# A small exp, its norm and its transpose taken one pass earlier in a fused attention and gated-MLP kernel

## Chip, cores, metric

The kernel runs on one core of one Trainium2 chip. The time is device time in microseconds (us) of that core; runs of each kernel are compared. The runs were made on several chips, so times are compared only within the same rounds, by their ratio. A span in a profile is about 1.8 us shorter than the time of the same run. Where a landing time of a DMA is given to 0.01 us, it is read from the records of the trace; the views round the time from issue to landing to 0.1 us.

The five engines are TensorE (PE, with weight loads as PEld), VectorE (DVE), ScalarE (ACT), GpSimd (POOL) and SyncE (SP), which here only issues DMAs. All DMAs of the part studied are issued by SP on one queue, which feeds 16 DMA engines.

## The reference

Attention without a softmax over scores: q is normalised over its 64 columns, k over the sequence, then two small products. The result, with the heads side by side, goes through a two-layer MLP with a scaled Silu.

```
q_s = softmax(q, axis=-1)                  # q, k, v: batch 8, heads 8, sequence 576, 64 columns
k_s = softmax(k, axis=sequence)
kv  = einsum('bhsd,bhse->bhde', k_s, v)
x   = einsum('bhsd,bhde->bhse', q_s, kv)   # turned into 4608 tokens x 512
h   = x @ w_in                             # 512 x 2048
out = (h * sigmoid(beta * h)) @ w_out      # 2048 x 512
```

## The kernel before

The 4608 tokens are worked off in nine slabs of 512. Slabs 0 to 7 are the first 512 rows of each batch. The 64 rows that remain of each batch (the "remaining queries", QRF when loaded, EQR after exp, QTR once transposed) are handled two batches at a time and gathered for slab 8. A slab has a first pass (`x @ w_in`, Silu on ScalarE, 64 matmuls) and a second pass (`@ w_out`, 64 matmuls). The attention of the next batch is slipped between these matmuls at fixed places: `spread(steps, a, b)` puts steps between the matmuls of positions a to b.

ScalarE needs one function table for Exp and one for Silu. So the exps of coming batches are bundled at the end of a first pass. The parts that the change touches:

```python
def load_qrem(b):                       # remaining queries of batches b and b+1
    i = b // 2 % 2
    for h in range(2):
        a = bass.AP(qt_h, (b + h)*H*S*D + SM*D, [[D, SR], [S*D, H], [1, D]])   # 256 B pieces
        add(SP, lambda e, h=h, a=a: e.dma_start(QRF[i][64*h:64*h+64, :, :], a), ...)

def load(b):
    load_main("qf", qt_h, QF, b); load_k(b); load_v(b)    # 1.05 + 1.18 + 1.18 MB
    if b % 2:
        load_qrem(b - 1)                                  # 0.26 MB

def exp_qr(pi):   ...   # ScalarE: EQR = exp(QRF)
def norm_rem(pi): ...   # VectorE: reduce, reciprocal, multiply
def tr_dma(pi):   ...   # SP: dma_start_transpose(QTR, EQR)

# slab 0, between the passes
load(2)
load_qrem(0)
...
# slab 0, end; slab 1's first matmuls are already mixed in
o2_evac(0, 2, 5, ACTE)
<Silu table load>
at(0, 0, 3); out_now(1, 2, 7, DVE); ...; out_now(1, 3, 7, DVE); at(2); at(3)
o2_evac(0, 3, 6, DVE)
store(0)
load(3)
# ... rest of slab 1's first pass: Silu on ScalarE ...
# slab 1, before the second pass
exp_qr(0)               # loads the Exp table
norm_rem(0)
tr_dma(0)
for b in (2, 3): exp_q(b); exp_k(b); ...
# slab 1, second pass: the remaining queries of batches 0 and 1 are used here
todo = spread(outr_steps(1), 101.5, 103) + attn_late(2)
```

`outr_steps(1)` are eight short matmuls that read QTR. They stand in TensorE's order, so TensorE waits there if QTR has not come.

The softmax here doesn't subtract the row's maximum and nothing guards it: scores larger than these inputs give would overflow.

## Time and profile before

| | before |
|---|---|
| median, first three runs | 285.29 us (284.43 to 285.29) |
| span of the profile | 283.1 us |
| TensorE busy | 275.2 us, 97% |
| TensorE's wait for QTR | one, near 68 us |

From the profile's page of the kernel before: the first part (busy us, share of the span, instructions) and the first line of the part on the chain of work that ended last.

```profile
PE 275.2 (97%) x1559; PEld 136.0 (48%) x1589; DVE 117.3 (41%) x218; ACT 178.6 (63%) x243; POOL 38.6 (14%) x57
...
PE 90%; ACT 4%; DMA 3%; issue 1%; DVE 1%; SPq 0%; ACTq 0%
```

TensorE is the limit almost everywhere. What can be won is only what TensorE loses in stalls. The chain of waits of the kernel before, from 55 to 71 us, shows the largest one left (columns: start in us, length in us, what).

```profile
55.05 4.28 PE PS L366 x19
...
60.05 1.28 ACT L322
...
61.35 0.64 ACT EQR L322
...
62.01 0.70 DVE QRS L340
...
62.97 0.69 DVE EQR L343
...
63.69 4.35 DMA QTR<-EQR
...
68.08 2.58 PE PS L366 x42
```

The chain leaves TensorE at 59 us, goes through the Exp table load, exp, norm and transpose, and returns to TensorE at 68.08. TensorE's timeline of the kernel before around that point (start, length, engine, line, operation, shapes, count, and the idle time before it):

```profile
64.76 2.75 PE L366 MATMUL PS<-WOUT,GT 128*128 128x512 bf16 x11
68.08 0.26 PE L366 MATMUL PS<-QTR,KVD 128*128 128x64 bf16 x3 [0.57 <-DMA QTR<-EQR]
```

The bracket counts idle time after the modelled end of the last matmul. Counted from start to start, where a matmul of 512 columns takes 0.216 us, the stall is 0.73 us. In what follows "stall" means this count. The SP queue and ScalarE of the kernel before, from their timelines:

```profile
33.42 0.43 SPq L249 DMA_DIRECT2D QF<-in_q_dram  x1
...
41.74 4.48 SPq L266 DMA_DIRECT2D QRF<-in_q_dram  x2
48.89 0.37 SPq L716 DMA_DIRECT2D out_dram<-O2S  x1
...
54.13 5.35 SPq L266 DMA_DIRECT2D QRF<-in_q_dram  x2
63.69 1.29 SPq L456 DMA_TRANSPOSE QTR<-EQR  x1
```

```profile
46.19 1.28 ACT L825 ACT_TABLE_LOAD   x1
...
48.87 3.58 ACT L642 ACTIVATE GT<-PS,BETA 128x512 bf16<-128x512 f32 x6 [1.18 <-PE PS L366]
```

ScalarE has 1.18 us to spare in front of slab 1's first Silu. On SP, the QRF load at 54.13 is the tail of load(3), and the transpose is next behind it. Load(3) landed at 67.47, the transpose at 68.03. Of the last piece of load(3), the QRF load issued at 57.20, the view of the QRF tile from 57.18 to 58 us says:

```profile
DMA to landing us min/median/max: 10.3/10.3/10.3
```

### The profile page before, as it was taken

Reading aid. Unit: us, or ns where it says so; the run is one execution under the profiler, and the core shown is the slowest. Engines: PE = TensorE matmul, PEld = TensorE weight load, DVE = VectorE, ACT = ScalarE, POOL = GpSimd, SP = SyncE. Lnnn points to the kernel's source line nnn. Section 1 sums busy time; section 2 is a strip of 40 time slices with the busy share of each in tenths; the row PEclk is TensorE's granted clock in tenths of the full one; section 3 lists DMA queues with packets and bytes.
Section 4 is the critical chain, followed back from the end, with each engine's and each line's share of the span. In section 5 each row is a group of like instructions: output and inputs, shape, how many; then the busy total and the mean of one; then the engine's idle time right before and its main releaser. Section 6 shows DMA issues by size and latency. Waiting matters only on the chain.

```text
span 283.1 us, 3884 instructions
## 1 busy us (share of the span) xinstructions
PE 275.2 (97%) x1559; PEld 136.0 (48%) x1589; DVE 117.3 (41%) x218; ACT 178.6 (63%) x243; POOL 38.6 (14%) x57
## 2 busy tenths in 40 slices
PE   7899999999999999999999999999999999999995
PEld 3545454444455445544554445444544444444443
DVE  4864886029781348124841473055705300110012
ACT  5968687999968926795579636892660076017500
POOL 6522041308021032100130000000000000000000
PEclk9999999999999999999999999999999999999999
DMA  7999999998998998217980033002500030012022
GB/s 243 375 391 400 389 387 378 347 382 138 336 322 251 362 365 285 39 35 252 375 102 1 0 150 74 2 1 100 141 2 0 9 141 0 0 54 96 0 74 74
DMA packets 41466, 50.07 MB, mean 177 GB/s; under 512 B 20324, under 2 KB 28772, under 8 KB 40296
## 3 DMA queue, kind: packets, MB, share of 16 engines
q1 hardware_dynamic: 40496, 48.77, 53.7%
q10 hardware_dynamic: 952, 1.06, 1.1%
q8 instruction: 12, 0.20, 0.3%
q14 instruction: 6, 0.05, 0.0%
HBM read 36.71 MB, written 9.44 MB: 163 GB/s over the span
## 4 chain that ended last, share of the span: by engine, by line
PE 90%; ACT 4%; DMA 3%; issue 1%; DVE 1%; SPq 0%; ACTq 0%
PE PS L366 89%; ACT EK L317 2%; DMA KF<-in_k_dram 2%; DMA QTR<-EQR 2%; ACT L322 0%; SPq L249 0%; PE PS L364 0%; ACT GT L642 0%; DVE QRS L340 0%; DVE EQR L343 0%; ACT VB L351 0%; ACT EQR L322 0%; ACT XT L530 0%; ACT O2S L710 0%; DVE O2S L731 0%
## 5 line engine op out<-in xcount | busy, mean ns | idle before, releaser
L642 ACT ACTIVATE GT<-PS,BETA 128x512 bf16<-128x512 f32 x144 | 96.6, 689 | 79.0 <-PE PS L366 79.0
L366 PE MATMUL PS<-WOUT,GT 128*128 128x512 bf16 (+2 forms) x579 | 131.4, 373 | 0.7 <-issue 0.2
L366 PE MATMUL PS<-XT,WIN 128*128 128x512 bf16 x561 | 131.2, 379 | 0.5
L366 PEld LDWEIGHTS PS<-XT,WIN 128*128 128x128 bf16 x576 | 60.1, 106 | 59.3 <-POOL WIN L566 0.5
L366 PEld LDWEIGHTS PS<-WOUT,GT 128*128 128x128 bf16 x592 | 55.3, 98 | 62.0 <-DVE O2S L710 0.2
L710 DVE COPY O2S<-PS 128x512 f32<-128x512 f32 x33 | 22.7, 687 | 107.7 <-PE PS L366 107.7
L366 PE MATMUL PS<-VB,EK 128*128 128x65 bf16 (+2 forms) x306 | 35.8, 191 | 1.2 <-ACT VB L351 0.7
L351 POOL CAST VB<-VF 128x576 bf16<-128x576 f32 x30 | 22.7, 757 | 76.5 <-DMA VF<-in_v_dram 47.1
L307 ACT ACTIVATE EK<-KF 64x1152 bf16<-64x1152 f32 x24 | 27.8, 1157 | 0.4
L366 PEld LDWEIGHTS PS<-VB,EK 128*128 128x128 bf16 x306 | 22.0, 98 | 8.1 <-ACT VB L351 0.8
L332 DVE TENSOR_REDUCE QS<-EQ 128x8 f32<-128x512 bf16 (+1 forms) x22 | 20.1, 913 | 3.1 <-ACT EQ L295 2.9
L441 DVE CAST XT<-PS 128x512 bf16<-128x512 f32 x24 | 16.4, 690 | 10.9 <-PE PS L366 10.9
L295 ACT ACTIVATE EQ<-QF 128x512 bf16<-128x512 f32 x32 | 17.9, 619 | 3.0 <-DMA QF<-in_q_dram 2.8
L334 DVE TENSOR_TENSOR EQ<-EQ,QI 128x1024 bf16<-128x1024 bf16 (+1 forms) x15 | 16.9, 1128 | 0.5
L366 PE MATMUL PS<-QT,KVD 128*128 128x512 bf16 x30 | 11.4, 379 | 0.0
L317 ACT ACTIVATE EK<-KF 64x576 bf16<-64x576 f32 (+1 forms) x12 | 9.9, 839 | 1.8 <-DMA KF<-in_k_dram 1.7
L334 POOL TENSOR_TENSOR EQ<-EQ,QI 128x512 bf16<-128x512 bf16 x7 | 7.3, 1042 | 18.5 <-DVE QI L333 18.2
L403 DVE TENSOR_TENSOR KVD<-PS,RC 64x64 bf16<-64x64 f32 (+2 forms) x28 | 8.6, 308 | 1.3 <-PE PS L364 0.5
L340 DVE TENSOR_REDUCE QRS<-EQR 128x8 f32<-128x512 bf16 x4 | 2.7, 678 | 13.2 <-ACT EQR L322 13.2
L366 PE MATMUL PS<-XT 128*128 128x512 f32 x10 | 6.7, 801 | 1.5 <-DVE XT L219 1.5
L642 ACT ACT_TABLE_LOAD x5 | 6.4, 1283 | 0.1
L295 ACT ACT_TABLE_LOAD x5 | 6.4, 1283 | 0.1
(52 smaller groups left out, 77.5 us busy)
## 6 DMA issues: line engine op xcount, KB each, us to landing
out_dram<-O2S SPq DMA_DIRECT2D x8, 1024.0 KB, 4.6
KF<-in_k_dram SPq DMA_DIRECT2D x6, 1152.0 KB, 8.2
VF<-in_v_dram SPq DMA_DIRECT2D x6, 1152.0 KB, 11.4
QF<-in_q_dram SPq DMA_DIRECT2D x6, 1024.0 KB, 6.8
KF<-in_k_dram SPq DMA_DIRECT2D x8, 288.0 KB, 8.1
VF<-in_v_dram SPq DMA_DIRECT2D x8, 288.0 KB, 8.7
WST<-in_moe_w_in_dram SPq DMA_DIRECT2D x8, 256.0 KB, 7.8
O2S<-in_moe_w_in_dram SPq DMA_DIRECT2D x4, 512.0 KB, 11.9
```

Of the source, the lines that this page charges most:

```text
L295: add(ACTE, lambda e, o=o, a=a: e.activation(o, a, ACT.Exp), r=[("qf", i, hp)], w=[("eq", i, hp)])
L307: add(ACTE, lambda e, o=o, a=a: e.activation(o, a, ACT.Exp), r=[("kf", i, h) for h in hps], w=[("ek", i, h, e_) for h in hps])
L317: add(ACTE, lambda e: e.activation(o, a, ACT.Exp), r=[("kf", i, h) for h in hps], w=[("ek", i, h, e_) for h in hps])
L332: add(DVE, lambda e: e.tensor_reduce(s_, a, AX.X, ALU.add), r=ks, w=[("qs", i, hp0)])
L334: add(eng, lambda e: e.tensor_tensor(a, a, vb, ALU.mult), r=ks + [("qi", i, hp0)], w=ks)
L340: add(DVE, lambda e: e.tensor_reduce(QRS[:, :], EQR[i][:, :, :], AX.X, ALU.add), r=[("eqr", i)], w=["qrs"])
L351: add(eng, lambda e: (e.copy if eng == ACTE else e.tensor_copy)(o, a), r=[("vf", i, hp), ("vone", i)], w=[("vb", i, hp, h) for h in ((0, 1 ...
L366: add(PE, lambda e: e.matmul(o, l, r_, start=start, stop=stop), r=r, w=w, bank=[bk])
L403: add(DVE, lambda e, o=o, a=a, s_=s_: e.tensor_tensor(o, a, s_, ALU.mult), r=[("ps", bk)] + [("rc", i, h) for h in hps], w=[("kvd", i, h, ...
L441: add(eng, lambda e: (e.copy if eng == ACTE else e.tensor_copy)(XT[i][:, hp, :], PS[bk][:, :]), r=[("ps", bk)], w=[("xt", i, hp)], bank=[bk])
L642: add(ACTE, lambda e: e.activation(GT[:, f, :], PS[bk][:, :], ACT.Silu, scale=BETA[:, f:f + 1]), r=[("ps", bk), "beta"], w=[("gt", f)], ba ...
L710: add(eng, lambda e: (e.copy if eng == ACTE else e.tensor_copy)(O2S[t % 2][:, u, :], PS[bk][:, :]), r=[("ps", bk)], w=[("o2", t % 2, u)], ...
```

## The change

The intent: the exp of the remaining queries of batches 0 and 1 no longer stands in front of the transpose in slab 1's second pass. It is taken earlier, while ScalarE still has the Exp table, so that norm and transpose can be done during slab 1's first pass. For that, the remaining queries must arrive earlier, so their load goes ahead of load(2).

```diff
             if t == 0:
+                load_qrem(0)
                 load(2)
-                load_qrem(0)
 ...
                 o2_evac(0, 2, 5, ACTE)
+                exp_qr(0)
                 <Silu table load>
 ...
                 o2_evac(0, 3, 6, DVE)
+                norm_rem(0)
                 store(0)
                 load(3)
+                tr_dma(0)
                 continue
 ...
             if t == 1:
                 nb = [2, 3]
-                exp_qr(0)
-                norm_rem(0)
-                tr_dma(0)
```

No instruction is added or dropped. On ScalarE the exp moves, on SP the two loads move; the order on TensorE, VectorE and GpSimd is the same.

## The prediction

> **What bounds the kernel now.** TensorE. The page has PE busy 275.2 us of a 283.1 us span (97%); the chain that ended last is 90% PE. From 20 us on, the starts of consecutive matmuls follow each other at their own pace (0.216 us for 512 columns; steps of double length are missing records). The stalls left are 0.1 us at 39.8, 0.1 at 53.08 (a PSUM bank waiting for Silu) and 0.73 us at 68.08, where the first QTR matmul waits for the transposed remaining queries.
>
> **What the change aims at.** That stall. In the chain of waits its path is: Exp table load at 60.05 (1.28 us), exp of EQR 61.35 (0.64), norm on VectorE 62.01 to 63.66, DMA transpose issued 63.69, landed 68.03 (4.35 us). The change takes exp, norm and issue out of this path. It can save at most 0.73 us, 0.26%.
>
> **Costs, from the trace.** No instruction is added: the orders show two moves, the 0.61 us exp on ScalarE and two QRF loads on the SP queue; both table loads (1.28 us) stay.
> - exp_qr(0) in front of the Silu table: ScalarE gets there at 46.19 and the first Silu waits until 48.87 for PE, with 1.18 us idle. The 0.61 us fits, with about 0.55 us to spare, if QRF has landed by about 46.7. QRF is now issued at 33.4; the transfer ahead of it landed at 43.92, and 1024 packets of 256 B add about 1 to 2 us (estimate from packets of 18 to 36 ns, 64 to an engine): about 45.3. No stall expected; beyond 46.7 PE pays in full: the bank wait at 53.08 has no slack.
> - norm_rem (1.65 us) falls into 13.2 us of VectorE idleness (48.9 to 62.0): free.
> - ScalarE's exps in slab 1's second pass start 0.6 us earlier, VectorE's norms about 1.7 us earlier, both transposes of batch 2 and load(4) likewise. No matmul waits for them now.
>
> **Why I expect little of the 0.73 us.** The transpose is still behind load(3) on the one SP queue. The Trainium skill (DMA: Bandwidth & Descriptors, section "Queues, rings and completion order") says each DMA engine consumes descriptors in ring order. The trace agrees: load(3)'s last piece (QRF of batch 2, issued 57.20) landed at 67.47 and the transpose 0.56 us later, though issued 3.8 us before that; packet records show the early engines' transpose packets held from 65.7 to 67.32, for the slowest engine. The fastest of these four transposes landed in 2.4 us, which would be 66.1. So the loads bound it, not its issue. After the change it is issued at about 59.5, when load(3) is issued, at the same place in the queue; the bytes ahead are the same, so it lands at about 67.5 to 68.1 again.
>
> **Predicted:** 284.9 us, 8 in 10 between 284.2 and 285.8 (before: runs 284.43 to 285.29). Faster by over 2%: 0.005; within 2%: 0.985; slower: 0.01.
>
> **What would show it.** QRF landing near 45 us and no ScalarE wait longer than before at 46 to 49; QRS right after O2S at 49 us; transpose issued near 59.5 with 8 us or more to landing; the QTR matmul still stalling 0.4 to 0.8 us near 68; batch 2's transposes issued 1.5 us earlier.
>
> **What would make it wrong.** The transpose passing the loads or the slowest DMA engine lagging less (up to 0.7 us gained); QRF landing after 46.7 us (loss); a transpose waiting early in the rings disturbing load(3).

## The result and the profile after

| | before | after |
|---|---|---|
| median of 6 runs | 285.24 us (284.43 to 285.64) | 285.50 us (284.94 to 286.02) |
| ratio after / before, 95% interval | | 1.0014 (0.9995 to 1.0034) |

A ratio is the mean time of one kernel's runs over that of the other's of the same rounds, so it is not quite the ratio of the medians. A second set (five rounds, `a_again` below) gave 1.0003 (0.9989 to 1.0018). The change brings nothing that can be told from zero.

The page of the kernel after, first and fourth part:

```profile
PE 276.1 (97%) x1559; PEld 136.3 (48%) x1589; DVE 117.2 (41%) x218; ACT 178.9 (63%) x243; POOL 38.5 (14%) x57
...
PE 94%; DMA 3%; issue 1%; ACT 0%; DVE 0%
```

The chain of waits after, 55 to 71 us:

```profile
59.73 0.69 ACT GT L642
...
60.48 8.45 DMA QTR<-EQR
...
68.98 2.08 PE PS L366 x32
```

Table load, exp and norm are gone from the chain. The stall is not: the one DMA now fills the whole stretch, 8.45 us from issue to landing where it was 4.35. The piece in front of it in the chain is only what SP happened to follow. TensorE's timeline after:

```profile
64.71 3.19 PE L366 MATMUL PS<-WOUT,GT 128*128 128x512 bf16 x13
68.98 0.20 PE L366 MATMUL PS<-QTR,KVD 128*128 128x64 bf16 x1 [1.09 <-DMA QTR<-EQR]
```

The stall, start to start, is 1.25 us. The SP queue, ScalarE and VectorE after:

```profile
33.84 4.24 SPq L266 DMA_DIRECT2D QRF<-in_q_dram  x2
38.12 2.69 SPq L249 DMA_DIRECT2D QF<-in_q_dram  x1
...
49.27 0.36 SPq L716 DMA_DIRECT2D out_dram<-O2S  x1
...
53.58 6.86 SPq L266 DMA_DIRECT2D QRF<-in_q_dram  x2
60.48 3.98 SPq L456 DMA_TRANSPOSE QTR<-EQR  x1
```

```profile
45.65 1.04 ACT L710 COPY O2S<-PS 128x512 f32<-128x512 f32 x2
46.77 0.63 ACT L322 ACTIVATE EQR<-QRF 128x512 bf16<-128x512 f32 x1
47.42 1.28 ACT L826 ACT_TABLE_LOAD   x1
...
49.25 3.00 ACT L642 ACTIVATE GT<-PS,BETA 128x512 bf16<-128x512 f32 x5 [0.33 <-PE PS L366]
```

```profile
49.27 0.69 DVE L340 TENSOR_REDUCE QRS<-EQR 128x8 f32<-128x512 bf16 x1
...
50.23 0.69 DVE L343 TENSOR_TENSOR EQR<-EQR,QRI 128x512 bf16<-128x512 bf16 x1
```

Everything moved as meant. The exp fits in front of the Silu table and the first Silu still waits for TensorE. The norm is done at 50.92 us. But SP comes to the transpose only after it has issued load(3), at 60.48, and the transpose then lands 0.57 us behind load(3)'s last piece (68.37). Before, it landed 0.56 us behind it. Of this last piece, issued at 58.11, the view of the QRF tile from 58.08 to 59 us says:

```profile
DMA to landing us min/median/max: 10.3/10.3/10.3
```

To compare profiles whose starts differ by some tenths of a microsecond, the table below counts from a fixed matmul, the last output product of batch 1 in slab 0 (47.15 us before, 47.53 us after). Where QTR is there in time, its first matmul starts 20.2 us after that point (20.20 and 20.21 us in four runs below without a wait).

| profile | order of the first QRF loads | load(2) and QRF ended | load(3) ended | QTR landed | stall, us |
|---|---|---|---|---|---|
| before | behind load(2) | 7.22 | 20.32 | 20.89 | 0.73 |
| b_again | behind | 6.90 | 19.62 | 20.21 | under 0.1 |
| after | ahead of load(2) | 7.82 | 20.84 | 21.41 | 1.25 |
| a_again | ahead | 7.54 | 20.48 | 21.02 | 0.86 |
| b_qrem_first | ahead | 7.60 | 20.67 | 21.27 | 1.11 |

From the fixed matmul to the end of the span, less this stall, the five profiles took 235.25 to 235.33 us. So behind this point the stall accounts for the difference between them to within 0.1 us. The part ahead of it varies by itself by 0.4 us (47.14 to 47.55), which also moves the times.

### The profile page after: what moved, and what is told of

Same layout as the page of the kernel before. It is cut to its first block, busy times and chain, and to the rows that moved or that the text cites. A ratio compares the mean times of both kernels' runs of the same rounds, so it can differ in the third digit from the quotient of the medians.

```text
span 284.0 us, 3884 instructions
## 1 busy us (share of the span) xinstructions
PE 276.1 (97%) x1559; PEld 136.3 (48%) x1589; DVE 117.2 (41%) x218; ACT 178.9 (63%) x243; POOL 38.5 (14%) x57
## 4 chain that ended last, share of the span: by engine, by line
PE 94%; DMA 3%; issue 1%; ACT 0%; DVE 0%
PE PS L366 93%; DMA QTR<-EQR 3%; PE PS L364 1%; ACT GT L642 0%; DVE XT L219 0%; DVE O2S L731 0%; DVE KVD L403 0%; ACT L295 0%
## 5 line engine op out<-in xcount | busy, mean ns | idle before, releaser
L351 POOL CAST VB<-VF 128x576 bf16<-128x576 f32 x30 | 22.7, 756 | 79.5 <-PE PS L366 49.9
L366 PE MATMUL PS<-XT 128*128 128x512 f32 x10 | 7.7, 908 | 1.5 <-DVE XT L219 1.5
L295 ACT ACT_TABLE_LOAD x6 | 7.7, 1283 | 0.1
L642 ACT ACT_TABLE_LOAD x5 | 6.4, 1283 | 0.1
L366 PE MATMUL PS<-QTR,KVD 128*128 128x64 bf16 x32 | 5.2, 193 | 1.1 <-DMA QTR<-EQR 1.1
```

Source lines behind the costliest of these rows:

```text
L295: add(ACTE, lambda e, o=o, a=a: e.activation(o, a, ACT.Exp), r=[("qf", i, hp)], w=[("eq", i, hp)])
L351: add(eng, lambda e: (e.copy if eng == ACTE else e.tensor_copy)(o, a), r=[("vf", i, hp), ("vone", i)], w=[("vb", i, hp, h) for h in ((0, 1 ...
L366: add(PE, lambda e: e.matmul(o, l, r_, start=start, stop=stop), r=r, w=w, bank=[bk])
L642: add(ACTE, lambda e: e.activation(GT[:, f, :], PS[bk][:, :], ACT.Silu, scale=BETA[:, f:f + 1]), r=[("ps", bk), "beta"], w=[("gt", f)], ba ...
```

## Experiments

Three explanations were on the table. *Queue order*: the transpose is held by the bytes queued ahead of it. *Issue*: its landing follows the moment it is issued. *Traffic*: a transpose must wait until load traffic on the DMA engines has ended, wherever it stands in the queue. Names beginning with a_ are edits of the changed kernel, those with b_ of the kernel before. One slip in the expectations: where they speak of batch 1's third output product as the fixed point, it is the fourth and last one; the numbers are those of the table above.

### The transpose ahead of load(3)

```diff
                 norm_rem(0)
+                tr_dma(0)
                 store(0)
                 load(3)
-                tr_dma(0)
```

> The changed kernel with one edit: the transpose of the remaining queries is put on the SP queue ahead of the store of slab 0 and of load(3), instead of behind them. Queue-order theory (the transpose is held by the bytes queued ahead of it): it is issued near 51 us, lands at 55 to 57.5 us behind load(2) alone, the QTR stall near 68 us (0.73 us before, 1.25 us after in the profiles) is below 0.1 us, and the time is 0.5 to 1.2 us under the changed kernel, about 284.5 us. Batch 2's own transposes, still behind load(3), become the next to wait for, but need not come before 71 us. Rival (a transpose has to wait until the load traffic on the DMA engines has ended, wherever it stands in the queue): it lands no earlier than about 67 us and the stall stays at 0.5 us or more. Second rival (a transpose among loads holds up the loads that follow): load(3) lands over 1 us later than 68.4 us.

Measured: 284.53 us (284.11 to 284.85), ratio to before 0.9979 (0.9962 to 0.9996), and 0.64 us under the changed kernel of the same rounds (285.17). The SP timeline of this kernel:

```profile
50.95 1.29 SPq L456 DMA_TRANSPOSE QTR<-EQR  x1
52.29 0.57 SPq L716 DMA_DIRECT2D out_dram<-O2S  x1
...
56.20 4.86 SPq L266 DMA_DIRECT2D QRF<-in_q_dram  x2
65.66 4.53 SPq L451 DMA_TRANSPOSE QT<-EQ  x2
```

The transpose landed at 55.66 us, 4.7 us after its issue, amid full load traffic and 0.38 us behind load(2)'s last piece (55.28), and the stall is gone: TensorE's waits no longer name QTR. So traffic alone does not hold a transpose until 68 us. The second rival came true as well: load(3) ended at 69.77 us, 1.4 us later than in the first profile after. No matmul waited for it. How much of that is the transpose and how much the store and loads issued 3 us later is not separated here. The same edit is not possible in the kernel before, whose exp comes too late for it.

### The changed kernel and the kernel before once more

> The changed kernel once more, unedited, for a second profile and timing beside the others. Queue-order theory: the transpose lands 0.4 to 0.7 us behind the last load(3) piece, wherever that falls; the stall follows the slowest DMA engine and lies between 0.4 and 1.5 us. Time 285.0 to 285.9 us, 0 to 0.3% over the kernel before. If the change itself had slowed something, the stall or another wait would again be larger than the 0.73 us of before.

Measured: 285.17 us (284.95 to 285.37), ratio 1.0003. Stall 0.86 us, the transpose 0.54 us behind load(3).

> The kernel before, unedited, for a second profile. Queue-order theory: the transpose lands 0.4 to 0.7 us behind the last piece of load(3) again; the stall differs from 0.73 us by no more than the landing of load(3) does. It shows how much of the difference between stalls of 0.73 and 1.25 us is chance.

Measured in one look: the transpose landed at 67.77 us, 0.59 us behind load(3) (67.18), and TensorE hardly waited (under 0.1 us). So the stall of the kernel before is itself a matter of some tenths: 0.73 us in one profile, nearly none in another. The landing behind load(3) is the fixed part: 0.49 to 0.60 us in the seven profiles that keep the whole of load(3) right ahead of the transpose.

### The QTR matmuls later in TensorE's order

```diff
-                todo = spread(outr_steps(1), 101.5, 103) + attn_late(2)
+                late = attn_late(2)
+                kv01, rest = late[:18], late[18:]
+                todo = spread([s for _, s in kv01[:17]], 101.5, 104) + \
+                    spread(outr_steps(1), 104.1, 105.4) + [(105.45, kv01[17][1])] + rest
```

They cannot go further down, because the 18th step is followed by writes to the KVD tile that they read.

> The kernel before with the QTR matmuls moved by about 1.1 us down TensorE's order (behind 17 of the 18 steps of batch 2's first two key-value products), nothing on other engines moved. If the stall near 68 us is nothing but a wait for the transpose's landing, TensorE gets to these matmuls at 68.2 us or later, the stall shrinks to below 0.3 us and the time falls by 0.4 to 0.7 us against the kernel before, to about 284.6 us. Rival (the wait only moves on: exps or transposes of batch 2 then come too late): a new stall of 0.4 us or more at the key-value or output products of batch 2 between 68 and 74 us, and no gain.

Measured: 284.34 us (284.24 to 284.48), ratio 0.9974 (0.9960 to 0.9989). TensorE's timeline of this kernel:

```profile
68.37 0.38 PE L366 MATMUL PS<-WOUT,GT 128*128 128x512 bf16 x1
68.58 0.34 PE L366 MATMUL PS<-QTR,KVD 128*128 128x64 bf16 x6
68.76 0.38 PE L366 MATMUL PS<-WOUT,GT 128*128 128x512 bf16 x1
```

The transpose landed at 67.50; TensorE came to it at 68.58 and did not wait. No new stall appeared. Of all kernels run here this one has the lowest ratio to the kernel before, without moving anything on another engine.

### Only the new order of loads

```diff
             if t == 0:
+                load_qrem(0)
                 load(2)
-                load_qrem(0)
```

> The kernel before with only the changed order of loads: the two loads of the remaining queries ahead of load(2); exp, norm and transpose stay where they were. In four profiles so far load(2) with these two loads ended 6.9 to 7.2 us after a fixed matmul (batch 1's third output product) where they came last, and 7.5 to 7.8 us where they came first, and load(3) ended 19.6 to 20.3 against 20.5 to 20.8 us after it. If the new order itself costs this load time (the many 256-byte packets slow the engine that lags), load(2) ends at 7.4 to 7.9 and load(3) at 20.3 to 20.9 us here too, and the stall is as after, 0.6 to 1.3 us, with a time of 0.0 to 0.2% over the kernel before. Rival (chance, or the earlier issue of the transpose behind load(3)): load ends as in the kernel before, stall 0 to 0.75 us.

Measured: 285.62 us (284.62 to 286.01), ratio 1.0025 (1.0006 to 1.0044). Load(2) with QRF ended at 7.60, load(3) at 20.67, stall 1.11 us. The time is a little more than the expected 0.0 to 0.2%. So the reordering of loads makes load(2) and load(3) end later by itself, with exp, norm and transpose left where they were. All twelve profiles agree: load(2) with QRF ended 6.90 to 7.37 us after the fixed matmul in the six of the old order, 7.44 to 7.82 in the six of the new one. For load(3), where the whole of it stood right ahead of the transpose on the one queue, it is 19.62 to 20.34 in four profiles of the old order and 20.48 to 20.84 in three of the new one, a gap of only 0.14 us. In the total time the cost is at the edge of the noise: the changed kernel, with the same order, gave 1.0014 and 1.0003. The stretches view (columns: stretch, its length, busy time of each engine with instruction counts, TensorE clock, DMA share, GB/s moved) of the kernel before, and of this one, over the same two stretches:

```profile
41.50:46.50 5.00, 4.95 (x39) 2.50 (x39) 3.35 (x10) 4.71 (x9) 1.33 (x2) 1.00 1.07 365
50.00:54.50 4.50, 4.50 (x22) 2.11 (x21) 0.00 (x0) 4.50 (x9) 0.66 (x1) 1.00 1.14 328
```

```profile
41.50:46.50 5.00, 4.95 (x39) 2.49 (x39) 3.35 (x10) 4.57 (x8) 1.33 (x2) 1.00 1.15 270
50.00:54.50 4.50, 4.50 (x22) 2.10 (x21) 0.00 (x0) 4.50 (x9) 0.00 (x0) 1.00 1.06 414
```

Wherever the QRF pieces of 256 bytes run, the last column falls: 365 to 270 GB/s when they come early, and in the second stretch 414 to 328 when they come late. The sums do not quite cancel: 3.30 MB moved before (365 x 5.0 + 328 x 4.5) and 3.21 MB here. The packet records of this run show other packets slowed beside them: from 42.0 to 44.5 us, in means of half a microsecond, those of 2304 bytes took 0.15 to 0.18 us in place of 0.10, and those of 1024 bytes 0.07 to 0.10 in place of 0.05. The last packets of 2304 bytes of load(2), with no 256-byte pieces beside them, took 0.09 (53.0 to 54.5 us). Why the loss is larger with QRF ahead than behind is not settled.

### The new exp without the new order of loads

```diff
             if t == 0:
-                load_qrem(0)
                 load(2)
+                load_qrem(0)
```

> The changed kernel without the reordering of loads: the remaining queries of batches 0 and 1 come behind load(2) again, while their exp stays in front of the Silu table. They land near 54 us, 7 us after the third output product of batch 1, so ScalarE waits from 46.2 to about 54 us in front of slab 1's first Silu, which starts near 56.5 us in place of 48.9. TensorE, whose PSUM banks have no slack here (0.1 us stall at 53.1 us already), loses 6.5 to 8 us: time 291 to 293.5 us, 2.2 to 2.9% slower. It shows what the reordering buys. If TensorE had slack in its eight banks, the loss would be under 5 us. The QTR stall is gone, as TensorE comes later.

Measured: 294.10 us (293.75 to 294.50), ratio 1.0325 (1.0309 to 1.0341), more than expected. ScalarE's timeline, TensorE's waits (us in total, times, longest) and three stretches of this kernel:

```profile
54.69 0.63 ACT L322 ACTIVATE EQR<-QRF 128x512 bf16<-128x512 f32 x1 [8.42 <-DMA QRF<-in_q_dram]
```

```profile
PE PS L366 <- ACT GT L642: 6.7, 2, 5.1
```

```profile
20.00:52.00 32.00, 31.61 (x187) 15.73 (x189) 19.63 (x46) 20.00 (x29) 6.38 (x7) 1.00 1.07 383
57.40:64.80 7.40, 5.54 (x13) 1.82 (x15) 0.00 (x0) 5.55 (x11) 0.00 (x0) 0.50 1.10 358
70.00:100.00 30.00, 29.78 (x205) 15.36 (x208) 19.35 (x36) 26.55 (x34) 9.53 (x11) 1.00 0.78 233
```

ScalarE waits 8.42 us for QRF, and TensorE, out of free PSUM banks, waits 6.7 us for Silu. The rest is the clock: when TensorE went on after 5.1 idle us, its granted clock was 0.50 for 7.4 us more, and matmuls started 0.43 us apart in place of 0.216. The 13 recorded ones cost about 2.7 us more (13 x 0.21, an estimate, as records can be missing). 6.7 and 2.7 give 9.4 us; the medians differ by 9.3. (The QTR stall, which is gone here, is not taken off, so the sum is good to some tenths only.) The Trainium skill (TensorE: Matmul & The Clock Gate, section "Part 1: The HAM clock gate (the "warmup" mystery)") says that an idle window of about 3.4 us halves the clock until TensorE has been busy for about as long. In this trace the clock record falls to 0.50 at 54.63 us, 2.3 us after the last matmul ended (52.37), which is sooner than that, though no matmul ran then to confirm it. It returns to 1.00 at 64.87, 3.9 us after matmuls went on at 60.93 behind a second idle piece of 1.6 us, which agrees. The early loads are thus a necessary part of the change.

### Fewer bytes ahead of the transpose

Both kernels were run without the load of V of batch 3, 1.18 MB ahead of the transpose (the expectations write 1.15). The result is wrong (batch 3 uses batch 1's V).

```diff
-            load_v(b)
+            if b != 3:
+                load_v(b)
```

> The changed kernel without the load of V of batch 3, 1.15 MB ahead of the transpose in the queue (a wrong result on purpose: batch 3 uses batch 1's V). Queue-order theory: everything behind it comes forward by the 2.8 to 3.2 us that these bytes take, so the transpose, issued near 60 us, lands at 65 to 66.2 us in place of 68.2 to 68.9, and the stall is gone. Rival (it lands when some other thing near 68 us frees it, not the bytes): it still lands after 67 us.

> The kernel before without the load of V of batch 3 (a wrong result on purpose, as above). Here the queue has emptied, or nearly, when the transpose is issued at 63.7 us, so now its issue decides: it lands 2.4 to 3 us after that, at 66.0 to 66.7 us, up to 1 us later than in the changed kernel without V. So the change does bring the landing forward where no backlog holds it. Rival (bytes do not matter): 67.5 us or later.

The SP lines of the view of the QTR tile between 45 and 75 us, with the time to landing, for the changed kernel and for the kernel before, each without V:

```profile
L457 SPq DMA_TRANSPOSE QTR<-EQR x1: 3477/3477/3477, 57.2 to 57.2; - x1
...
DMA to landing us min/median/max: 7.6/7.6/7.6
```

```profile
L457 SPq DMA_TRANSPOSE QTR<-EQR x1: 1291/1291/1291, 63.7 to 63.7; - x1
...
DMA to landing us min/median/max: 2.5/2.5/2.5
```

In the changed kernel the transpose landed at 64.85 us, 0.57 us behind load(3), which ended at 64.28. It was issued early and still waited for what was ahead. In the kernel before the queue had emptied at 64.27, and the transpose landed at 66.19, 2.5 us after its issue. Here the issue decides, and by itself the change does bring the landing forward, by 1.2 us counted from the fixed matmul (17.79 against 19.02). Both stalls are gone, and both landings are those of the queue-order theory to within 0.2 us of the stated ranges. This is the case that the change was made for; with V loaded it does not arise.

### The transpose on ScalarE's queue

```diff
-        def tr_dma(pi):
+        def tr_dma(pi, eng=SP):
 ...
                 load(3)
-                tr_dma(0)
 ...
                 nb = [2, 3]
+                tr_dma(0, ACTE)
```

Batch 2's first transpose also waits for QTR here, so that no two transposes from different queues are under way at once.

> The changed kernel with the transpose of the remaining queries issued by ScalarE on its own queue, at the end of slab 1's first pass (about 60.2 us, as late as in the changed kernel), instead of behind load(3) on the SP queue; batch 2's first transpose waits for it, so that no two are under way at once. Queue-order theory (its place in the SP queue holds it, not the traffic as such): it passes what is left of load(3), lands at 63 to 66 us, and the QTR stall near 68 us is gone; time 0.3 to 1.2 us under the changed kernel, less up to 1 us if the issue holds up ScalarE's exps of batch 2. Rival (a transpose needs all 16 DMA engines to have finished the loads under way, from whichever queue): it lands no earlier than 67 us and the stall stays at 0.4 us or more.

Measured: 284.95 us (284.77 to 285.12), ratio to before 1.0010 (0.9995 to 1.0025). From the view of the QTR tile of this kernel:

```profile
L457 ACTq DMA_TRANSPOSE QTR<-EQR x1: 1485/1485/1485, 59.5 to 59.5; - x1
...
DMA to landing us min/median/max: 8.2/8.2/8.2
```

Neither expectation was met in full. The landing came as late as the rival had it (67.70 us), but it was ahead of load(3)'s end (68.49), so the transpose did pass the tail of the SP queue. It needed 8.2 us for that, and the stall shrank to 0.23 us, between the two expectations. No gain in time is to be seen: the ratio is no better than the changed kernel's 1.0014 and 1.0003 of other rounds. The packet records show where the 8.2 us went. The transpose's first packet ran at 63.77 us, 4.2 us after its issue (1.3 us in the kernel before without V, where the queue was empty); what held it until then is open. Then several of its packets were held at once and released together, as if the transpose went on only when a slower DMA engine had caught up (in this profile they are the only packets of ScalarE's queue at that time; columns: start us, bytes, us, end us):

```
64.40  256  0.578  64.98
64.47  256  0.524  65.00
64.51  256  0.469  64.98
```

The kernel before shows the same on the one queue, packets of 256 bytes and semaphore writes of 4 bytes held until one instant:

```
65.68  256  1.640  67.32
65.69    4  1.631  67.32
65.76  256  1.558  67.32
66.11  256  1.201  67.32
66.56    4  0.754  67.32
```

With no transpose under way, no 256-byte packet of the QRF loads took over 0.08 us (1024 packets in the kernel before, 49.9 to 54.2 us). So "queue order" is too simple by itself. The reading that fits is that the transpose waits for the slowest of the 16 DMA engines to come through what is ahead of it, and that on another queue this engine still carries its share of the loads. It is not shown: the packet records do not name the DMA engine. The prediction's words "for the slowest engine" are the same reading.

### The loads of the next remaining queries behind the transpose

```diff
-            if b % 2:
+            if b % 2 and b != 3:
                 load_qrem(b - 1)
 ...
                 norm_rem(0)
                 tr_dma(0)
+                load_qrem(2)
```

> The kernel before with only the two loads of the remaining queries of batches 2 and 3 (262 KB in 256-byte packets) moved behind the transpose in the SP queue. Queue-order theory: the transpose lands 0.4 to 0.7 us behind the V load of batch 3, which now is the last ahead of it, 0.3 to 0.6 us earlier than in the kernel before (19.3 to 20.5 us after batch 1's third output product, where it was 20.2 to 20.9), and the stall is 0 to 0.35 us; time 0 to 0.5 us under the kernel before. Rival (the issue decides): it lands as before.

Measured: 284.34 us (284.31 to 284.39), ratio 0.9989 (0.9973 to 1.0006). The V load of batch 3 landed at 65.69 and the transpose at 66.21, 0.52 us behind it and 19.07 us after the fixed matmul; there is no stall. This is a little earlier than expected, since V itself came earlier without small packets beside it (18.55 us after the fixed matmul; 19.75, 18.86 and 19.18 in three profiles with them). As 66.21 is also 2.5 us after the issue, the issue and the queue now bind alike.

## Why the prediction was right

- **What bounds the kernel, and what can be won.** Right. The only stall at stake was the one on QTR. The two edits that removed it in five rounds gained 0.21 and 0.26%, against a predicted ceiling of 0.26%.
- **The transpose stays behind load(3), so little is won.** Right, and shown from both sides: issued 3.6 us earlier, counted from the fixed matmul, it still landed 0.57 us behind load(3) (0.56 before); put ahead of load(3) it landed at 55.66; with 1.18 MB taken out ahead of it, it came forward with the loads. The prediction named "passing the loads" as what could make it wrong; when it passed their tail on another queue, 0.23 us of the stall were left.
- **"The bytes ahead are the same, so it lands at about 67.5 to 68.1 again", stall 0.4 to 0.8 us.** The mechanism was right, this term was mis-sized. The landing was at 68.94 and 68.22, the stall 1.25 and 0.86 us. The same bytes took longer in the new order: the run with nothing but that order had load(3) end at 20.67 us after the fixed matmul (19.62 to 20.34 in four profiles of the old order) and a stall of 1.11 us. The prediction had counted the reordering as free.
- **QRF lands at about 45.3 us.** Too early: 46.69 and 46.02 in two profiles. The transfer ahead of it already landed 0.9 us later than before, once the shift of the profile is taken off. ScalarE was free at 46.69 in the first profile, so the exp began at 46.77 and nothing was lost, but the margin, put at 1.4 us (45.3 against 46.7), was down to the 0.33 us that the first Silu still waited for TensorE (0.65 in the second profile).
- **Beyond 46.7 us TensorE pays in full.** Right in kind, not quite in full: with the old order of loads QRF landed at 54.60 us, 7.9 us past this point, and TensorE waited 6.7 us. The half clock after it, 2.7 us more, was not foreseen.
- **Norm and exp are free where they go.** Right: the Silu after them still waited 0.33 us for TensorE, and VectorE did the norm in an idle stretch.
- **Batch 2's transposes 1.5 us earlier.** The first was issued 1.6 us earlier after the shift (65.65 against 66.83), the second about 1.0. It was worth nothing, as said.
- **The time.** 284.9 predicted, 285.5 measured, within the stated 284.2 to 285.8. The small gain that was expected did not come; the stall it would have come from grew by the cost of the load order. That the time fell into the range says little by itself: the range is 1.6 us wide, more than twice the most that could be won, and also holds the kernel before. What tests the prediction is the landing behind load(3), not the time.

The versions that beat both kernels are those that take the stall away where it arises. Moving eight matmuls by 1.1 us gave 284.34 us against 284.94 for the kernel before in the same rounds (0.9974), and moving the transpose ahead of the loads gave 284.53. Both gains are small but their intervals lie under 1.

## What to carry to other kernels

Before moving the work that prepares a DMA, look at what is queued ahead of that DMA: if it lands a constant time behind the transfer in front of it, an earlier issue gains nothing, and only its place in the queue, the bytes ahead or the place of its consumer will. Reordering loads of the same bytes was not free here, where two of them consist of 256-byte pieces that slow the transfers beside them; why one order costs more than the other stays open. Where a wait is under a microsecond, moving the consumer down its own engine's order can be the cheapest remedy.

## What the Trainium skill lacked or had wrong

- DMA: Bandwidth & Descriptors, section "DMA Transpose (X-bar)": it does not say that packets of a transpose can be held while loads are under way. Section "Queues, rings and completion order" says that each DMA engine consumes descriptors in ring order, which agrees with landings 0.49 to 0.60 us behind the load ahead, and that data descriptors carry no barrier. Here packets of 256 and of 4 bytes were held for up to 1.64 us and all released at 67.32 us.
- The same page, section "Why small descriptors are slow (HBM only)": it speaks of the small transfer itself. Here the loads in pieces of 256 bytes also slowed others' packets, 2304 bytes from 0.10 to 0.15 us and more, 1024 bytes from 0.05 to 0.07 us and more, and the rate over 5 us fell from 365 to 270 GB/s.
- ScalarE: Activation LUTs, section "What ACT_TABLE_LOAD costs": it gives about 1283 ns for the load, which the trace shows (1.28 us), and about 1380 ns of drain with it, 2.66 us for a switch. In the profile after, exp ended at 47.40 us, the load ran from 47.42 to 48.70 and the next activation began at 48.71: about 1.3 us in all, with no drain to be seen.
- No page says for this chip why a transpose issued on ScalarE's queue, while load(3) was under way on the SP queue, ran its first packet only 4.2 us after its issue (59.52 to 63.77 us).
